# Normalizing x without the modulation, and folding scale and shift into the DFT over the hidden dimension

## The chip, the cores and the metric

The kernel runs on one core of a Trainium2 chip. Its time is the device time of the program in microseconds, the median of the runs shown. Before the change three runs gave 1993.35, 1994.33 and 1990.18 us, median 1993.35. The engines are called TensorE (PE, with its weight loads as PEld), VectorE (DVE), ScalarE (ACT), GpSimd (POOL) and SyncE (SP), as in the profile.

## What is computed

```python
# x 2048 x 1024 (S x D), w_mod 1024 x 6144, w1 1024 x 3584, w2 3584 x 1024, DFT matrices S x S and D x D
sa, ca, ga, sb, cb, gb = (silu(c) @ w_mod) in six rows of 1024
h = LN(x) * (1 + ca) + sa
x = x + ga * A(h)          # A(h) = Re(DFT over the sequence of (DFT over the hidden dimension of h))
h = LN(x) * (1 + cb) + sb
x = x + gb * (gelu(h @ w1 + b1) @ w2 + b2)
# A(h) = Wsre @ (h @ Wdre.T) - Wsim @ (h @ Wdim.T), with the four DFT matrices given as fp32 inputs
```

Everything is fp32, and the result has to be close to fp32 in accuracy.

## The kernel before, in words

**Stages.** The sequence DFT is done first (real and imaginary part of S @ h), then the DFT over d, then the two products of the MLP. TensorE works in f16: each fp32 operand is scaled by a power of two and split into a high and a low half, and each product is three passes, high by high, high by low and low by high. The high half is a cast by ACT, the low half a subtraction by DVE. Nearly all large products use a Strassen-like scheme of seven products on combined quarter blocks, so that DVE and POOL also form sums and differences of operands.

In the order of the program on TensorE:

- The start. The rows sa and ca are made by TensorE as fp32 matmuls: for each eighth k of d, four 128 x 512 products of the column silu(c), repeated 128 times, with a 1 MB piece of w_mod (`mod_pe`, L474; the last eighth in `mod_rows`, L486). Between them stand idle f16 matmuls (`idle_pe`, L480). From the rows DVE takes a maximum and a power-of-two scale (L507 to L511).
- The first stage, called plain (L1112): 16 chunks of 48 matmuls, 768 in all, the products of the first sequence-DFT quadrants with the x tiles. Chunk n = 8 ri + kp needs matrix chunk n (`c0_tasks`, split by L681 on ACT and L684 on DVE) and the halves of the x tiles.
- The second stage (L1162): 84 operands of 24 matmuls, the rest of the sequence DFT, on sums of x tiles (`s_tasks`) and sums of matrix chunks (`comb_c`, L716, split again by L681/L684).
- The third stage (L1394): the DFT over d, 1344 matmuls on the results u of the stages before and on the seven combinations of each DFT matrix over d (`d_tasks`), which go through DRAM as dc (store L828, reload `load_dp` L1359).
- The two products of the MLP (L1585, L1694), 2352 matmuls each.

**Work on x.** `x_tasks(k)` handles the tiles k and k + 8 of 128 rows: mean and variance (bn_stats on DVE for k = 0, sums on ACT for the others, L592, L601, L605), the inverse root with a Newton step on two-column tiles (L603 to L618), then for each tile (x - mean) * ca1 (L633), times r plus sa (L634), the cast (L635, ACT) and the low half (L636, DVE). Tile 0 goes through `mod_rows` by halves of 512 columns (L494, L499, L504), since it is first.

**Other rows.** `row_tasks` makes ga, sb, cb and gb on DVE in the second stage: eight loads of 512 KB, eight products with the column silu(c) accumulated in one tile (L542 for the first, L544 for the others), then an all-reduce over the partitions on POOL (L552) and a store.

**Matrices over d.** `d_tasks(n)`, n = 0 to 7, follows the rows: a 1 MB load of two row blocks (L810), split and combined in place (high half L821 on ACT with the scale SD = 16, low half L824 on DVE, differences L837, L841, L842), and stored by POOL (L828) through a ring of four staging tiles.

**What sets the order.** Each piece of such work is a Task with an engine, a modelled cost and dependencies, in one of several streams, each with a due time. While the kernel is built, `pick` and `fill_to` choose the task that can start first by modelled clocks (`clk`, `done`, `LANDS`), up to the modelled time of TensorE, whose matmuls are written out in order; `need` and `emitted` force what a matmul reads. The chip executes each engine's list in exactly that order. T0 is the modelled time at which the first stage starts. All loads are issued by SP in order, on eight completion semaphores in turn, so at most eight are outstanding; POOL issues the stores of s, u and dc.

## Time and profile before

| | |
|---|---|
| median of the runs | 1993.35 us (1990.18 to 1994.33) |
| profiled execution, its span | 1990.4 us; it lies 2.95 us under the median and inside the range of the runs |
| TensorE busy in it | 1969.1 us, 99% |
| first matmul of the first stage | 47.42 us |
| start of the second stage (L1162) | 221.68 us |
| start of the third stage (L1394) | 658.33 us |
| DVE, ACT, POOL busy | 1417.3, 851.1, 190.5 us |

A page of the profile gives in its first part the busy time of each engine, in the second the same by 40 slices of the span, in the fourth the chain of work that ended last, in the fifth the costliest groups of instructions (`line engine operation out<-in xcount | busy, mean ns of one | idle time of the engine just before them, and what ended most of it`). A row of the timeline is `start, length, engine, line, operation, count [idle before <-releaser]`. The granted clock of TensorE was 1.00 in the second stage.

### The profile page before, as it was taken

The numbers are of one execution on the slowest core, as the hardware profiler recorded it, in microseconds if no ns is written. First come the engines' busy times: TensorE is split into PE (matmuls) and PEld (weight loads), VectorE is DVE, ScalarE is ACT, GpSimd is POOL, SyncE is SP. The second block draws the span as 40 slices with busy tenths as digits, with TensorE's granted clock in tenths as the row PEclk, the third lists the DMA queues.
The fourth block names the chain that finished last, engine by engine and source line by source line (L and its number), as shares of the span: only waits on it lengthen the run. The fifth ranks groups of instructions, "written<-read, shape, count | busy, mean of one in ns | idle before, by whom it ended". The sixth has DMA issues, their size and how long they took to land. (4 is left out here: it accounts for less than half of the span.)

```text
span 1990.4 us, 23735 instructions
## 1 busy us (share of the span) xinstructions
PE 1969.1 (99%) x9082; PEld 896.5 (45%) x9082; DVE 1417.3 (71%) x1795; ACT 851.1 (43%) x1091; POOL 190.5 (10%) x282
## 2 busy tenths in 40 slices
...
DVE  2977886997984467777588999999873353553566
...
GB/s 380 53 97 281 236 264 275 246 298 329 249 256 364 271 261 256 282 244 277 276 218 190 171 199 168 145 175 146 169 231 216 117 97 83 127 101 69 111 74 85
DMA packets 139363, 402.42 MB, mean 202 GB/s; under 512 B 15536, under 2 KB 15536, under 8 KB 134640
## 3 DMA queue, kind: packets, MB, share of 16 engines
...
HBM read 262.95 MB, written 137.89 MB: 201 GB/s over the span
## 5 line engine op out<-in xcount | busy, mean ns | idle before, releaser
L1694 PE MATMUL ps<-arena 128*128 128x512 f16 x2352 | 511.1, 379 | 2.8 <-DVE arena L1740 1.5
L1585 PE MATMUL ps<-arena 128*128 128x512 f16 x2352 | 510.2, 379 | 2.2 <-ACT arena L1607 2.2
L1162 PE MATMUL ps<-arena 128*128 128x512 f16 x2016 | 435.5, 379 | 1.4 <-DMA arena<-s 1.4
L1694 PEld LDWEIGHTS <-arena 128*128 128x128 f16 x2352 | 229.9, 98 | 281.5 <-issue 3.8
L1585 PEld LDWEIGHTS <-arena 128*128 128x128 f16 x2352 | 230.1, 98 | 279.4 <-issue 2.5
L1740 DVE SCALAR_TENSOR_TENSOR arena<-ps,i4c,arena 128x1024 f32<-128x1024 f32 x179 | 229.3, 1281 | 144.4 <-PE ps L1694 143.1
L1162 PEld LDWEIGHTS <-arena 128*128 128x128 f16 x2016 | 197.1, 98 | 239.5 <-DMA arena<-s 1.9
L1394 PE MATMUL ps<-arena 128*128 128x512 f16 x1344 | 292.4, 379 | 1.9 <-DMA arena<-u 1.9
L386 ACT ACTIVATE arena<-arena,shc 128x512 f16<-128x512 f32 (+1 forms) x115 | 115.9, 1018 | 277.3 <-PE ps L1694 184.6
L1394 PEld LDWEIGHTS <-arena 128*128 128x128 f16 x1344 | 131.4, 98 | 158.0 <-DMA arena<-u 2.4
L1112 PE MATMUL ps<-arena 128*128 128x512 f16 x768 | 167.4, 379 | 7.2 <-ACT arena L635 2.0
L411 DVE TENSOR_TENSOR arena<-arena 128x512 f32<-128x512 f32 (+1 forms) x228 | 171.0, 753 | 4.1
L681 ACT ACTIVATE arena<-arena 128x1024 f16<-128x1024 f32 x100 | 104.1, 1050 | 150.8 <-PE ps L1162 111.4
L398 DVE SCALAR_TENSOR_TENSOR arena<-arena,shc 128x512 f16<-128x512 f32 (+1 forms) x115 | 128.7, 1122 | 38.4 <-ACT arena L386 38.3
L684 DVE SCALAR_TENSOR_TENSOR arena<-arena 128x1024 f16<-128x1024 f32 x100 | 128.6, 1303 | 18.5 <-ACT arena L681 18.5
L1611 DVE TENSOR_TENSOR arena<-arena,ps 128x512 f32<-128x512 f32 x84 | 57.5, 685 | 110.7 <-PE ps L1585 106.5
L1604 ACT ACTIVATE arena<-arena,b1s,i1c 128x512 f32<-128x512 f32 x84 | 68.3, 813 | 137.0 <-DVE arena L1611 137.0
L1112 PEld LDWEIGHTS <-arena 128*128 128x128 f16 x768 | 74.7, 98 | 99.9 <-ACT arena L635 4.0
L773 ACT ACTIVATE arena<-arena 128x1024 f16<-128x1024 f32 x56 | 57.7, 1047 | 60.9 <-DVE arena L1186 18.8
L776 DVE TENSOR_TENSOR arena<-arena 128x1024 f16<-128x1024 f32 x56 | 66.9, 1218 | 14.6 <-ACT arena L773 14.6
L386 ACT ACTIVATE arena<-arena,s1c 128x512 f16<-128x512 f32 (+1 forms) x70 | 60.8, 884 | 36.9 <-DVE arena L411 25.9
L398 DVE SCALAR_TENSOR_TENSOR arena<-arena,s1c 128x512 f16<-128x512 f32 (+1 forms) x70 | 66.3, 959 | 11.0 <-ACT arena L386 10.8
...
## 6 DMA issues: line engine op xcount, KB each, us to landing
...
arena<-w SPq DMA_DIRECT2D x119, 256.0 KB, 2.7
...
arena<-u SPq DMA_DIRECT2D x112, 256.0 KB, 4.0
...
```

The costliest lines, as they stand in the source:

```text
L386: act.activation(o[m][0], q(j), AF.Copy, **sc)
L398: dve.scalar_tensor_tensor(o[m][1], q(j), scale, o[m][0], op0=ALU.mult, op1=ALU.subtract)
L411: dve.tensor_tensor(q(d), q(a), q(b), op=op)
L681: h = Task("act", 1.15, lambda: act.activation(o[:, :, 0], s2, AF.Copy, scale=SC), list(deps) + free)
L684: dve.scalar_tensor_tensor(o[:, :, 1], s2, SC, o[:, :, 0], op0=ALU.mult, op1=ALU.subtract)
L1112: pe.matmul(bank_of(d_), hleft(d_, s, kp, a), cop(n)[:, s, b], start=(kp == 0 and s == 0 and a == 0 and b == 0), stop=(kp == 7 and s == 1 ...
L1162: pe.matmul(bank_of(st + ch), left, cop(n)[:, s, b], start=(start and kp == 0 and s == 0 and a == 0 and b == 0), stop=(kp == 3 and s == 1 ...
L1394: pe.matmul(bank_of(bk), up(N)[:, c_, a], dp(n)[:, c_, w], start=(start and ri == 0 and c_ == 0 and i == 0), stop=(ri == 1 and c_ == 3 and ...
L1585: pe.matmul(ps.rearrange("p (k t) -> p k t", k=4), w1c[:, m, s, a, d * P : (d + 1) * P], zc(m)[:, b, :, d, :], start=(start and d == 0 and ...
L1604: act.activation(dst, src, AF.Gelu_apprx_tanh, scale=inv, bias=b1s[:, 2 * p + j : 2 * p + j + 1])
L1694: pe.matmul(t[:, j], hidc[:, c_, m, a, k * P : (k + 1) * P], w2c[:, m, c_, w], start=(start and c_ == 0 and n == 0), stop=(c_ == 1 and n = ...
L1740: lambda: dve.scalar_tensor_tensor(dst, ps[b], inv, dst, op0=ALU.mult, op1=ALU.add), kp[b],
```

## The change

The rows sa and ca no longer scale x. LN(x) alone, times 128, is split and goes through the sequence DFT (one TENSOR_SCALAR for each tile, L624), and its column 0 is overwritten with the constant 128 (a memset of one column, L625). So column 0 of the product holds the row sums of the sequence matrices. The scale is put into the matrices over d: each row block d is multiplied by cs[d] = (1 + ca[d]) times a power of two, and from it the term of row 0 is taken off (`d0`, two scalings per matrix chunk, L817), since column 0 of LN(x) was dropped; LN(x) sums to zero over d, so that this column is minus the sum of the others. Row 0 of the matrix over d is replaced by the row A0 or A1, the product of sa with the matrix (`arow_d`, a 4 KB load into one partition).

With that go these edits:

- `mod_pe`, `mod_rows`, their eight 1 MB loads and 32 fp32 matmuls are taken out; 18 idle matmuls stay ahead of the first stage. T0, the modelled start, is 9 where it was 42. SP's first loads are those of x and of the sequence matrix.
- bn_stats on DVE are used for k = 0 and 1.
- ca, sa and ga are made by `row_tasks` (products L490, L492, all-reduce L501) during the first stage, in places of the u area; after ca and sa follow a few operations that turn each row into a column (L508, L511, L516) and make the scales (L520 to L527). `need("early")` stands ahead of the last chunk.
- In the second stage the rows are sb, A0, A1, cb, gb, five where there were four (ga, sb, cb, gb); A0 and A1 use pieces of the matrices over d and the column of sa.
- `d_tasks` takes its chunks in the order 1, 2, 3, 0; each is scaled by two SCALAR_TENSOR_TENSORs (L817) before it is split, SD is 8, the high half is a plain cast (L833), the low half a TENSOR_TENSOR (L836), and the staging ring has three tiles.

SP's list at the start of the program, before (cc is the vector c, wm is w_mod, cre the real part of the sequence matrix; `arena` is one large on-chip buffer in which all tiles lie):

```order
L1433 DMA cc_187<-in_c_dram 128x8
L1427 DMA arena_65<-in_wm_dram 128x2048 x7
L1424 DMA arena_65<-in_x_dram 128x1024 x2
L1427 DMA arena_65<-in_wm_dram 128x2048
L692 DMA arena_65<-in_cre_dram 128x2x512
L1424 DMA arena_65<-in_x_dram 128x1024 x2
L692 DMA arena_65<-in_cre_dram 128x2x512 x2
L1424 DMA arena_65<-in_x_dram 128x1024 x2
L692 DMA arena_65<-in_cre_dram 128x2x512
L1424 DMA arena_65<-in_x_dram 128x1024 x10
```

and now:

```order
L1444 DMA cc_189<-in_c_dram 128x8
L1438 DMA arena_65<-in_x_dram 128x1024 x2
L686 DMA arena_65<-in_cre_dram 128x2x512
L1438 DMA arena_65<-in_x_dram 128x1024 x2
L686 DMA arena_65<-in_cre_dram 128x2x512
L1438 DMA arena_65<-in_x_dram 128x1024 x2
L686 DMA arena_65<-in_cre_dram 128x2x512
L1438 DMA arena_65<-in_x_dram 128x1024 x2
L686 DMA arena_65<-in_cre_dram 128x2x512
L1438 DMA arena_65<-in_x_dram 128x1024 x8
L483 DMA arena_65<-in_wm_dram 128x1024 x4
```

The weights stand behind all of x and four matrix chunks, and in pieces of half the size.

DVE's list in the start before (ps is the product of the modulation rows; L684 is the low half of the first matrix chunk, L504 the low half of half a tile of x):

```order
L507 TENSOR_REDUCE mx_189<-ps 128x1 [waits PE_49] x4
L508 TENSOR_REDUCE m_5_188<-mx_189 128x1 [waits DVE_49]
L199 TENSOR_SCALAR m_5_188<-m_5_188 128x1 [waits DVE_49]
L510 RECIPROCAL m_5_188<-m_5_188 128x1 [waits DVE_49]
L511 TENSOR_SCALAR m_5_188<-m_5_188 128x1 [waits DVE_49]
L494 SCALAR_TENSOR_TENSOR arena_65<-arena_65,xmv_9_192,ps 128x512
L514 SCALAR_TENSOR_TENSOR xcl_10_193<-xcl_10_193,m_5_188 128x2 [waits DVE_49]
L499 SCALAR_TENSOR_TENSOR arena_65<-arena_65,xcl_10_193 128x512 [waits DVE_49,Activation_49]
L603 TENSOR_SCALAR xcl_12_195<-xmv_11_194 128x2
L684 SCALAR_TENSOR_TENSOR arena_65<-arena_65 128x2x512 [waits DMAHW3_49]
L504 TENSOR_TENSOR arena_65<-arena_65 128x512 [waits DMAHW5_49,Activation_49]
```

and now, from the end of the statistics of the first pair of tiles (L624 and L625 are the new normalization, L630 the low half of an x tile, L678 that of a matrix chunk, L490 the first product of the row ca):

```order
L624 TENSOR_SCALAR arena_65<-arena_65,xmv_11_196,xcl_12_197 128x1024 [waits DVE_49]
L625 MEMSET arena_65 128x1 [waits DVE_49]
L587 BN_STATS xst_10_195<-arena_65 128x6 [waits DMAHW4_49]
L490 TENSOR_SCALAR arena_65<-arena_65,scol_188 128x1024 [waits DMAHW5_49]
L630 TENSOR_TENSOR arena_65<-arena_65 128x2x512 [waits Activation_49]
L678 SCALAR_TENSOR_TENSOR arena_65<-arena_65 128x2x512 [waits DMAHW3_49]
L624 TENSOR_SCALAR arena_65<-arena_65,xmv_11_196,xcl_12_197 128x1024
L625 MEMSET arena_65 128x1 [waits DVE_49]
L598 TENSOR_SCALAR xcl_16_201<-xmv_15_200 128x2 [waits Activation_49]
L587 BN_STATS xst_10_195<-arena_65 128x6
```

The maximum over the rows and the scaling by halves are gone. The product L490, which waits for a load of SP, stands between the normalization of the first x tile and the low halves of that tile and of the first matrix chunk.

DVE's list at the first unit of the matrices over d before (L824 is the low half, L837 a difference of two quarters, L776 the split of u, L716 a sum of matrix chunks):

```order
L684 SCALAR_TENSOR_TENSOR arena_65<-arena_65 128x2x512 [waits PE_49]
L824 SCALAR_TENSOR_TENSOR arena_65<-arena_65 128x512 [waits DMAHW6_49,DMASW7_49,Activation_49]
L824 SCALAR_TENSOR_TENSOR arena_65<-arena_65 128x2x512 [waits DMASW1_49,DMASW0_49,Activation_49]
L837 TENSOR_TENSOR arena_65<-arena_65 128x512
L837 TENSOR_TENSOR arena_65<-arena_65 128x512 [waits DVE_49]
L776 TENSOR_TENSOR arena_65<-arena_65 128x4x2x128 [waits DMASW6_49]
L776 TENSOR_TENSOR arena_65<-arena_65 128x4x2x128 [waits DMASW2_49,Activation_49]
L716 TENSOR_TENSOR arena_65<-arena_65 128x1024
L684 SCALAR_TENSOR_TENSOR arena_65<-arena_65 128x2x512 [waits PE_49]
```

and now (L817 scales, L836 is the low half, L849 the difference, L678 the low half of an operand of the second stage):

```order
L678 SCALAR_TENSOR_TENSOR arena_65<-arena_65 128x2x512 [waits PE_49,Activation_49] x2
L817 SCALAR_TENSOR_TENSOR arena_65<-arena_65,cs_190 128x1024 [waits DMAHW5_49]
L817 SCALAR_TENSOR_TENSOR arena_65<-arena_65,cs_190 128x1024
L678 SCALAR_TENSOR_TENSOR arena_65<-arena_65 128x2x512 [waits PE_49,Activation_49]
L836 TENSOR_TENSOR arena_65<-arena_65 128x2x512 [waits DMASW5_49,Activation_49]
L836 TENSOR_TENSOR arena_65<-arena_65 128x512 [waits DMASW7_49,Activation_49]
L849 TENSOR_TENSOR arena_65<-arena_65 128x512
L849 TENSOR_TENSOR arena_65<-arena_65 128x512 [waits DVE_49]
```

DVE's first operation of a unit now waits for the load itself (DMAHW); before, ACT's cast did so, and DVE waited for ACT.

The diff, cut to its core:

```diff
-SD = 16.0
+ONE = 1.0
+SD = 8.0
...
-    O_ROW = (72, 76)
-    O_DS = (O_AUX + 8, O_AUX + 12, 64, 68)
+    O_ERLY, O_LATE = (184, 188, 192, 196), (O_AUX, O_AUX + 4, O_AUX + 8, O_AUX + 12)
+    O_D0 = O_AUX + 12
+    O_DS = (O_AUX + 8, 64, 68)
...
+    def row_tasks(name, places, after):
+
+        mrow = at(places[0], 1024)
+        src = {"A0": 0, "A1": 1}
         r = []
         for k in range(ND):
-            b = at(O_AUX + 4 + 4 * (k % 3), 1024)
-            l = Task(
-                "dma", 1.5, lambda k=k, b=b: sp.dma_start(b, wm[:, k, j * D : (j + 1) * D]),
-                [("row", j, k - 3) if k > 2 else ("row", j - 1, ND) if j > 2 else ("op", 15)], ("wm", j, k),
-            )
+            b = at(places[1 + k % 3], 1024)
+
+            def load(k=k, b=b):
+                if name in src:
+                    sp.dma_start(b, dri[src[name]][:, k, :])
+                else:
+                    j = ("sa", "ca", "ga", "sb", "cb", "gb").index(name)
+                    sp.dma_start(b, wm[:, k, j * D : (j + 1) * D])
+
+            l = Task("dma", 1.5, load, [("row", name, k - 3)] if k > 2 else [after] if after else [], ("wm", name, k))
+            col = csa if name in src else scol
...
+            deps = [l.key] + ([("row", "sa", "end")] if name in src else [])
...
+        def column(o):
+
+            def f():
+                dve.tensor_tensor(rows, rows, ident[:, None, :].to_broadcast([P, ND, P]), op=ALU.mult)
+
+            def g():
+                dve.tensor_reduce(o, rows, axis=AX.X, op=ALU.add)
+
+            return [("dve", 1.25, f), ("dve", 1.25, g)]
...
+            dve.tensor_scalar(cs, cs, sd, None, op0=ALU.mult)
+            dve.tensor_scalar(m1[:, 4:5], m1[:, 4:5], sd, -1.0, op0=ALU.mult, op1=ALU.mult)
+            dve.tensor_scalar(csa, csa, sd, 1.0 / ONE, op0=ALU.mult, op1=ALU.mult)
...
-        if k < 1:
+        if k < 2:
...
-            mean, op = (mv[:, n, 0:1], ALU.subtract) if k < 1 else (ss[:, n : n + 1], ALU.add)
+            mean, op = (mv[:, n, 0:1], ALU.subtract) if k < 2 else (ss[:, n : n + 1], ALU.add)
+
+            def norm(x_=x_, mean=mean, op=op, n=n):
+                dve.tensor_scalar(x_, x_, mean, r[:, n : n + 1], op0=op, op1=ALU.mult)
+                dve.memset(x_[:, 0:1], ONE * SH)
+
             u = chain(
-                ("dve", 1.3, lambda x_=x_, mean=mean, op=op: dve.scalar_tensor_tensor(x_, x_, mean, ca1s, op0=op, op1=ALU.mult)),
-                ("dve", 1.3, lambda x_=x_, n=n: dve.scalar_tensor_tensor(x_, x_, r[:, n : n + 1], sas, op0=ALU.mult, op1=ALU.add)),
+                ("dve", 0.8, norm),
...
-        ri, c_ = divmod(n, 4)
+        ri, c_ = n // 4, (1, 2, 3, 0)[n % 4]
         b = at(O_AUX, 2048).rearrange("p (h x) -> p h x", h=2)
         q = at(O_AUX, 2048).rearrange("p (q e) -> p q e", q=4)
-        l = Task("dma", 2.9, lambda: sp.dma_start(b, dri[ri][:, c_::4, :]), [("dd", n - 1)] if n else [("row", 5, ND)])
+        d0 = at(O_D0, 1024)
+        l = Task("dma", 2.9, lambda: sp.dma_start(b, dri[ri][:, c_::4, :]), [("dd", n - 1)] if n else [("row", "gb", "end")])
         LANDS[l.key] = 5.0
+        head = [l]
+        if n % 4 == 0:
+            z = Task("dma", 1.5, lambda: sp.dma_start(d0, dri[ri][0, 0].partition_broadcast(P)), l.deps)
+            w = Task("dve", 0.7, lambda: dve.tensor_scalar(d0, d0, m1[:, 4:5], None, op0=ALU.mult), [z.key], ("d0", ri))
+            head += [z, w]
+        got = []
+        for h in range(2):
+
+            def f(h=h):
+                k = c_ + 4 * h
+                dve.scalar_tensor_tensor(b[:, h], b[:, h], cs[:, k : k + 1], d0, op0=ALU.mult, op1=ALU.add)
+
+            head.append(Task("dve", 1.3, f, [l.key, ("d0", ri)]))
+            got.append(head[-1].key)
+        if c_ == 0:
+            head.append(Task("dma", 0.3, lambda: sp.dma_start(b[0:1, 0, :], arow_d[ri][:, :]), [got[0], ("row", f"A{ri}", "end")]))
+            got[0] = head[-1].key
...
-                act.activation(o[0][:, :, 0], q[:, sl], AF.Copy, scale=SD)
+                act.activation(o[0][:, :, 0], q[:, sl], AF.Copy)
 
             def lo():
-                dve.scalar_tensor_tensor(o[0][:, :, 1], q[:, sl], SD, o[0][:, :, 0], op0=ALU.mult, op1=ALU.subtract)
+                dve.tensor_tensor(o[0][:, :, 1], q[:, sl], o[0][:, :, 0], op=ALU.subtract)
...
-    T0 = 42.0
+    T0 = 9.0
...
+                if ri and kp == 7 and s == 0 and d == 0:
+                    need("early")
...
+    for k in range(8):
+        for i in (k, k + 8):
+            load_x(i).run()
+            done["x", i] = 4.0 + 1.4 * (2 * k + i // 8 + min(k, 4))
+        if k < 4:
+            c0[k][0].run()
+            done["craw", k] = 4.0 + 1.4 * (3 * k + 2)
...
+    idle_pe(18)
+    clk.update(dma=8.0, act=4.0, dve=1.5, pe=8.0)
...
-    for n, j in enumerate((2, 3, 4, 5)):
-        push("row", "row", row_tasks(j, {2: "ga", 3: "sb", 4: "cb", 5: "gb"}[j]), t_op(16) + 20.0 + 30.0 * n)
+    last = None
+    for n, name in enumerate(("ca", "sa", "ga")):
+        push("row", "early", row_tasks(name, O_ERLY, last), t_op(6) + 30.0 * n)
+        last = ("row", name, "end")
...
+    for n, name in enumerate(("sb", "A0", "A1", "cb", "gb")):
+        push("row", "row", row_tasks(name, O_LATE, last), t_op(16) + 10.0 + 24.0 * n)
+        last = ("row", name, "end")
```

178 lines of the change are left out of this document (57 added, 121 removed).

## The prediction

> **What bounds the kernel now.** I read the page from the top: its first part (busy time of each engine), DVE's row of the second (busy tenths in 40 slices), and in the fifth the group of the first DFT stage.
>
> ```profile
> PE 1969.1 (99%) x9082; PEld 896.5 (45%) x9082; DVE 1417.3 (71%) x1795; ACT 851.1 (43%) x1091; POOL 190.5 (10%) x282
> ...
> DVE  2977886997984467777588999999873353553566
> ...
> L1112 PE MATMUL ps<-arena 128*128 128x512 f16 x768 | 167.4, 379 | 7.2 <-ACT arena L635 2.0
> ```
>
> TensorE is busy for all but 21.3 us of the 1990.4 us span. Every later stage hides its preparation, so time can be gained only where TensorE is busy with something that is no product of the DFTs, and that is the start. The timeline of PE shows it, with the starts of the later stages:
>
> ```profile
> 7.13 1.96 PE L474 MATMUL ps<-arena 128*128 128x512 f32 x4 [0.17 <-DMA arena<-in_wm_dram]
> 39.91 3.60 PE L486 MATMUL ps<-arena 128*128 128x512 f32 x8
> 47.42 0.39 PE L1112 MATMUL ps<-arena 128*128 128x512 f16 x1 [0.24 <-ACT arena L517]
> 64.70 62.75 PE L1112 MATMUL ps<-arena 128*128 128x512 f16 x290 [1.07 <-DVE arena L684]
> 221.68 93.40 PE L1162 MATMUL ps<-arena 128*128 128x512 f16 x432
> 658.33 42.03 PE L1394 MATMUL ps<-arena 128*128 128x512 f16 x194
> ```
>
> From 7 to 43.5 us TensorE makes the modulation rows; the first product of the sequence DFT starts at 47.42. The 290 matmuls take 62.75 us, 0.2164 each. All 768 of that stage at this pace are 166.2 us, and it ends at 221.68: it runs as if it had started at 55.5, so 8.1 us of waits lie behind 47.42. The third stage (L1394) starts 436.65 us after the second (L1162).
>
> **The change, the start.** The 8 MB of modulation weights no longer come first, and L474, L486 and the scaling that depends on them are gone; x and the DFT matrix lead the queue. When data land, the timeline of DVE and ACT tells, by the first instructions that waited for them:
>
> ```profile
> 23.21 1.29 DVE L592 BATCH_NORM_STATS2 xst<-arena 128x6 f32<-128x512 f32 x2 [21.77 <-DMA arena<-in_x_dram]
> 28.33 1.06 ACT L681 ACTIVATE arena<-arena 128x1024 f16<-128x1024 f32 x1 [1.76 <-DMA arena<-in_cre_dram]
> 29.70 1.06 ACT L601 ACTIVATE arena<-arena 128x1024 f16<-128x1024 f32 x1 [0.31 <-DMA arena<-in_x_dram]
> ```
>
> These are the 15th, 19th and 20th half megabyte of the queue (each 1 MB load of weights counts two): 1.30 us for each, with a lead of 23.21 - 15 x 1.30 = 3.7 us. So after the change the first tile of x is there near 5, its partner near 6.3, the first chunk of the matrix near 7.6, and high halves could feed TensorE from about 12 us. That alone would start the stage some 35 us sooner.
>
> But the order of DVE's work shows one instruction in the way: the first product of the row ca (L490) stands ahead of the low half of the first x tile (L630) and of the first matrix chunk (L678), and it reads the 21st half megabyte, which lands at 29.70 + 1.30 = 31.0. DVE executes in order. Behind L490 are both low halves that the second and third pass of the first chunk need; TensorE can do a handful of high-by-high products and then waits. I therefore start DVE's ramp at 31.0, not at 12.
>
> The Trainium skill, page "DMA: Bandwidth & Descriptors", section "Where 436 GB/s comes from", says that loads from HBM are bound near 358 GB/s per core. By that, 21 x 0.524 MB would land at 3.7 + 30.8 = 34.5, and the sum below would be 3.5 us later; the rows above say 1.30 us per 0.524 MB, 403 GB/s, and I go by them.
>
> What DVE must do from there until the low half of x tile 4 is out is counted from its order and priced by the groups by form of the first 700 us:
>
> ```profile
> L542 DVE TENSOR_SCALAR arena<-arena,scol 128x1024 f32<-128x1024 f32 x4 | 3.0, 748 | 10.0 <-DMA arena<-in_wm_dram 10.0
> L544 DVE SCALAR_TENSOR_TENSOR arena<-arena,scol 128x1024 f32<-128x1024 f32 x28 | 35.8, 1280 | 19.4 <-DMA arena<-in_wm_dram 19.3
> L636 DVE TENSOR_TENSOR arena<-arena 128x1024 f16<-128x1024 f32 x15 | 18.4, 1223 | 3.5 <-ACT arena L635 3.5
> L592 DVE BATCH_NORM_STATS2 xst<-arena 128x6 f32<-128x512 f32 x4 | 2.5, 671 | 21.8 <-DMA arena<-in_x_dram 21.8
> L615 DVE TENSOR_TENSOR xcl<-xcl 128x2 f32<-128x2 f32 x8 | 1.3, 158 | 0.1
> L647 DVE TENSOR_TENSOR arena<-arena 128x512 f32<-128x512 f32 x8 | 5.5, 683 | 0.0
> L634 DVE SCALAR_TENSOR_TENSOR arena<-arena,xcl 128x1024 f32<-128x1024 f32 x15 | 19.2, 1282 | 0.3
> L635 ACT ACTIVATE arena<-arena 128x1024 f16<-128x1024 f32 x15 | 15.8, 1056 | 22.7 <-DVE arena L634 22.7
> L716 DVE TENSOR_TENSOR arena<-arena 128x1024 f32<-128x1024 f32 x48 | 62.4, 1307 | 4.4 <-DMA arena<-s 4.1
> ```
>
> Eight products for ca: 0.75 + 7 x 1.28 = 9.7. Nine low halves of x and five of the matrix at 1.22: 17.1. Nine normalizations, now one TENSOR_SCALAR each (0.75 by L542, the same form) and a one-column memset (at most a small operation, so below 0.16; I take 0.06): 7.3. Three statistics with their aggregation: 2.2. Some 37 operations on two columns at 0.16: 5.9. One subtraction at 0.69. Together 42.9 us. For comparison the removed pair L633/L634 cost 2.56 per tile, so the lighter normalization is counted in this, 1.75 saved on each tile.
>
> In that stretch lies the all-reduce of ca on POOL. What an all-reduce does to DVE, the timeline shows where one was running:
>
> ```profile
> 244.55 6.69 DVE L684 SCALAR_TENSOR_TENSOR arena<-arena 128x1024 f16<-128x1024 f32 x2
> 244.74 7.02 POOL L552 PARTITION_ALL_REDUCE arena<-arena  x1 [22.79 <-DVE arena L544]
> ...
> 342.02 7.01 POOL L552 PARTITION_ALL_REDUCE arena<-arena  x1 [34.16 <-DVE arena L544]
> 342.98 5.55 DVE L716 TENSOR_TENSOR arena<-arena 128x1024 f32<-128x1024 f32 x1
> ```
>
> An operation of 1.21 us (that is what L716 takes alone; its mean of 1.307 above includes the stretched ones) took 5.55 beside it, and two of about 1.25 took 6.69: I charge 4.35 for each all-reduce (bounds: 0, if nothing of DVE's falls beside it, to 7.0, all of it). Waits of DVE for ACT's high halves I take at 2.5 (L636 waited 3.5 in all before; 0 to 4). Ramp: 31.0 + 42.9 + 4.35 + 2.5 = 80.8. The first four chunks are 4 x 48 = 192 matmuls and two more run on the high half, so 574 x 0.2164 = 124.2 us follow: 205.0. The all-reduces of sa and ga stand in POOL's order among the stores of the sums s, whose reload the last chunks and the second stage wait for, each 7.0 us long; I add 1.5 (0 to 4). The second stage starts at 206.5 instead of 221.68: **-15.2**. Lower end of the time: no block and no waits by ACT, then the first chunk itself sets the pace, DVE delivering two low halves at 31.0 + 0.75 + 2 x 1.22 = 34.2 and the stage running as if begun at 35: 201.5, -20. Upper end: 4 for the stores and 2.5 more for the block, -10.
>
> **The change, the second stage.** Here TensorE has no gap to lose, and the question is whether DVE still keeps up:
>
> ```profile
> 380.00:440.00 60.00, 60.00 (x280) 27.20 (x279) 58.74 (x53) 30.40 (x32) 15.52 (x21) 1.00 0.66 240
> 440.00:500.00 60.00, 60.00 (x280) 27.20 (x279) 49.71 (x49) 26.71 (x28) 10.53 (x20) 1.00 0.91 340
> 500.00:560.00 60.00, 60.00 (x280) 27.20 (x279) 53.95 (x55) 32.38 (x35) 15.32 (x29) 1.00 0.67 238
> 560.00:620.00 60.00, 60.00 (x280) 27.20 (x279) 43.62 (x40) 23.90 (x25) 7.00 (x13) 1.00 0.84 302
> ```
>
> (Span, then busy time of PE, PEld, DVE, ACT, POOL.) DVE's busy time is 206.0 of 240 us; 34.0 are free. Added: 16 scalings of the matrices over d as STT, 20.5; two of the term d0, 1.5; one row more than before (five for four), 9.7, with its block 4.35. Sum 36.1, 2.1 over what is free there. It also inherits waits: the loads of these matrices were waited for by ACT, by the view of waits
>
> ```profile
> ACT arena L821 <- DMA arena<-in_dre_dram: 10.3, 3, 4.0
> ACT arena L821 <- DMA arena<-in_dim_dram: 7.4, 2, 6.9
> ```
>
> 17.7 us, and now by L817 on DVE, with low halves of the stage's own operands queued behind it (L678, for TensorE's next pieces, and u). If all of it stays bare: 2.1 + 17.7 = 19.8. If the rows spread into the free time before 380, nothing is left: 0. I take **+5**, near the low end, since in the order two low halves (2.4 us) stand between most loads' issue and L817, and before 380 there is room as well: in DVE's digits above (slices of 49.8 us), the fifth to seventh, 199 to 348, read 8, 8 and 6. The patched row (a 4 KB load) and the smaller staging ring (three buffers for four) are costed at nothing: the units are 24 us apart, and the stores they wait for land within that.
>
> The chain of rows and units must also end in time for the third stage. Before:
>
> ```profile
> 226.87 0.74 DVE L542 TENSOR_SCALAR arena<-arena,scol 128x1024 f32<-128x1024 f32 x1
> 358.80 0.75 DVE L542 TENSOR_SCALAR arena<-arena,scol 128x1024 f32<-128x1024 f32 x1 [0.46 <-DMA arena<-in_wm_dram]
> 396.14 0.56 SPq L810 DMA_DIRECT2D arena<-in_dre_dram  x1
> 565.70 0.55 SPq L810 DMA_DIRECT2D arena<-in_dim_dram  x1
> 587.33 1.22 DVE L824 SCALAR_TENSOR_TENSOR arena<-arena 128x1024 f16<-128x1024 f32 x1
> ```
>
> Rows start 44.0 apart, the last takes 37.3, units are 24.2 apart, the last ends 22.9 after its load; all done 69.8 us ahead of 658.33. After: first row 5.2 behind 206.5, then 4 x 44.0 + 37.3 + 7 x 24.2 + 22.9 gives 617; with 2.6 more per unit, 638. The third stage would start at 206.5 + 436.65 + 5 = 648. The slack shrinks from 70 to between 10 and 31 us; the reload of the products takes some of it, but I charge nothing here.
>
> **Sum.** 1990.4 - 15.2 + 5.0 = 1980.2 for a profiled execution; the median before lies 2.95 above that of its profile, so 1983.2, **1983**. Its own range: the start alone (-20 to -10) moves it to 1978 or 1988, the second stage alone (0 to 10) likewise; with part of both, 1976 to 1990.
>
> **The rivals.** One of them needs the products' way out and back, from the DMA part for the first 700 us (KB each, median us from issue to landing):
>
> ```profile
> dc<-arena POOLq DMA_DIRECT2D x56, 256.0 KB, 4.4
> arena<-dc SPq DMA_DIRECT2D x14, 1024.0 KB, 10.4
> ```
>
> A, the held product does not hold (its weights land early, or the low halves do not wait behind it). Then the stage runs as if begun near 20 (12 plus some 8 us of waits, as before): 20 + 166.2 + 1.5 = 187.7, -34, sum 1990.4 - 34 + 5 + 2.95 = 1964. Against it: DVE's order, and a queue that is in order.
> B, the block of the all-reduce and the second stage cost nothing: -20 + 0, sum 1973. For it: DVE's free time before 380, and that the block hits only an operation which happens to meet it. Against: at both all-reduces shown DVE's work was stretched by over 4 us.
> C, the second stage is DVE's: 10 to 20 us of the 19.8 come bare, sum 1988 to 1998, middle 1993, no change. For it: 58.74 busy of 60 in the first of the four windows, at the very place of the first units.
> D, slower: the third stage waits for the last products of the scaled matrices. Mechanism: each unit now waits on DVE for its load (17.7 / 8 = 2.2) and scales (2.6), 29.0 apart instead of 24.2; last unit done at 206.5 + 5.2 + 213.3 + 7 x 29.0 + 22.9 + 4.8 = 656, with 4.4 for the store and 10.4 for the reload near 671 against 643: 28 us of wait, sum 1990.4 - 15.2 + 28 + 2.95 = 2006. It decides from the point where chain and reload end more than 19 us behind 643. Against: the slack of 70 us of before, and that the planner may pack the units closer than 24.2 when they are due.
>
> **Chances.** Forecast 0.58, A 0.05, B 0.14, C 0.14, D 0.09. This kernel's measurement can tell about 0.2%, 4 us, from no change: within it is 1989.4 to 1997.3. Faster: forecast, A, B and a third of C, 0.81. Same: most of what is left of C, 0.10. Slower: D, 0.09. For the range, 1973 to 1994 holds the forecast, most of B and two thirds of C.
>
> **What would show it.** Right: DVE idle from about 11 to 31 us, released by the weights' load ahead of L490; TensorE's second burst of L1126 near 34; the first all-reduce near 70 with a DVE operation of some 5.5 us beside it; a wait of TensorE of about 4 us at chunk 4, near 80; L1176 from about 206; L1408 from 642 to 650. Wrong: no idle DVE ahead of L490 (A); L1176 after 212 (ramp underpriced); idle PE in L1176 with L678 as releaser (C); a wait at L1408 for the reload of dc, which the last unit's stores release (D).

## The result

The changed kernel takes 2010.32 us (median of four runs, 2005.9 to 2012.6) against 1992.19 us of the kernel before on the same chip: a ratio of 1.009, 95% interval 1.0073 to 1.0107. It is slower by 18 us; the prediction had it faster by 10. The profiled execution of the changed kernel has a span of 2010.8 us.

The page of the changed kernel, part 1 and the TensorE groups of part 5:

```profile
PE 1943.2 (97%) x8978; PEld 882.8 (44%) x8978; DVE 1463.0 (73%) x1854; ACT 843.6 (42%) x1078; POOL 224.2 (11%) x286
...
L1176 PE MATMUL ps<-arena 128*128 128x512 f16 x2016 | 442.1, 382 | 17.7 <-DVE arena L678 11.5
...
L1408 PE MATMUL ps<-arena 128*128 128x512 f16 x1344 | 292.9, 379 | 6.6 <-ACT arena L1424 4.1
...
L1126 PE MATMUL ps<-arena 128*128 128x512 f16 x768 | 173.8, 390 | 32.8 <-DVE arena L678 23.5
```

TensorE does 26 us less work, and waits 46 us more. 25.6 of these stand in the first stage (32.8 against 7.2), where they were forecast. The others are new: the second stage, which had waited 1.4 us, waits 17.7, most of it for low halves (L678), and the third waits 6.6 where it had waited 1.9. The timeline of PE in the changed kernel shows where (start, length, count, and in brackets the wait ahead of it with its releaser):

```profile
14.02 1.89 PE L1126 MATMUL ps<-arena 128*128 128x512 f16 x4 [6.46 <-ACT arena L629]
36.04 42.55 PE L1126 MATMUL ps<-arena 128*128 128x512 f16 x188 [20.13 <-DVE arena L678]
81.25 1.04 PE L1126 MATMUL ps<-arena 128*128 128x512 f16 x2 [2.66 <-ACT arena L629]
82.51 116.38 PE L1126 MATMUL ps<-arena 128*128 128x512 f16 x527 [0.23 <-DVE arena L630]
202.25 11.99 PE L1126 MATMUL ps<-arena 128*128 128x512 f16 x47 [3.37 <-DVE arena L678]
214.08 93.62 PE L1176 MATMUL ps<-arena 128*128 128x512 f16 x433
309.46 98.58 PE L1176 MATMUL ps<-arena 128*128 128x512 f16 x456 [1.76 <-DVE arena L678]
410.51 22.35 PE L1176 MATMUL ps<-arena 128*128 128x512 f16 x95 [2.47 <-DVE arena L678]
433.94 5.35 PE L1176 MATMUL ps<-arena 128*128 128x512 f16 x24 [1.08 <-DMA arena<-s]
441.54 12.44 PE L1176 MATMUL ps<-arena 128*128 128x512 f16 x49 [2.25 <-DMA arena<-s]
459.27 151.98 PE L1176 MATMUL ps<-arena 128*128 128x512 f16 x695 [5.30 <-DVE arena L678]
...
673.76 26.06 PE L1408 MATMUL ps<-arena 128*128 128x512 f16 x120
```

Three differences make up the 20.4 us between the two spans. The first stage ends at 214.08 instead of 221.68: -7.6. The second takes 673.76 - 214.08 = 459.7 instead of 436.65: +23.0. From the third stage's start to the end it is 2010.8 - 673.8 = 1337.0 instead of 1332.1: +5.0.

The 23.0 are more than the added waits of 16.3. Most of the difference is the pace after a wait: the 456 matmuls behind the wait of 1.76 us take 98.58 us, 0.2162 each, but the 49 behind the wait of 2.25 take 12.44, 1.85 more than 49 x 0.2162, the 95 behind 2.47 take 1.81 more, and the 695 behind 5.30 take 1.72 more. The mean granted clock was 0.987 in this run, 0.999 in the one before. The Trainium skill, page "TensorE: Matmul & The Clock Gate", section "Part 1: The HAM clock gate (the "warmup" mystery)", says that the clock falls to half after an idle window of about 3.4 us, and comes back after a busy one of that length. An estimate from that is half of 3.4 us, 1.7, for the burst behind a wait, near the 1.8 measured; but here waits from 2.25 us on paid it, and not every one did (a wait of 3.73 us in the third stage of e4, below, cost 0.13).

The start went as the prediction described it. DVE and POOL in the changed kernel:

```profile
12.82 0.06 DVE L625 MEMSET arena<- 128x1 f32 x1
32.96 0.75 DVE L490 TENSOR_SCALAR arena<-arena,scol 128x1024 f32<-128x1024 f32 x1 [19.48 <-DMA arena<-in_wm_dram]
33.63 1.22 DVE L630 TENSOR_TENSOR arena<-arena 128x1024 f16<-128x1024 f32 x1
34.76 1.22 DVE L678 SCALAR_TENSOR_TENSOR arena<-arena 128x1024 f16<-128x1024 f32 x1
...
71.20 6.99 POOL L501 PARTITION_ALL_REDUCE arena<-arena  x1 [61.69 <-DVE arena L492]
72.12 5.03 DVE L641 TENSOR_TENSOR arena<-arena 128x512 f32<-128x512 f32 x1
```

One product of the row ca holds DVE for 19.5 us, with both low halves behind it. What it waited for came at 32.96, 2 us after the 31.0 reckoned from the rows of before. The 34.5 that followed from the Trainium skill's page "DMA: Bandwidth & Descriptors" (section "Where 436 GB/s comes from") was too late by 1.5; 32.96 lies between the two. The all-reduce stretches a 0.69 us operation to 5.03.

The end of the first stage had a wait that was not forecast. POOL and DVE ahead of the last chunk:

```profile
188.77 2.21 POOL L659 DMA_DIRECT2D s<-arena  x4 [12.14 <-DVE arena L655]
191.01 6.81 POOL L501 PARTITION_ALL_REDUCE arena<-arena  x1
...
197.85 0.76 DVE L554 TENSOR_SCALAR arena<-arena,m 128x1024 f32<-128x1024 f32 x1 [6.01 <-POOL arena L501]
...
200.98 1.22 DVE L678 SCALAR_TENSOR_TENSOR arena<-arena 128x1024 f16<-128x1024 f32 x1
```

The all-reduce of ga stands in POOL's list behind four stores, so it starts at 191; DVE waits 6.0 us for it at L554, and the low half of the last matrix chunk is behind that. TensorE loses 3.4 us and then 1.8 by the clock. (What the all-reduce itself does there, without this dependency, e7 shows below.)

### The profile page after: what moved, and what is told of

Read it like the earlier page. It is cut to its first block, busy times and chain, and to the rows that moved or that the text cites. A ratio compares the mean times of both kernels' runs of the same rounds, so it can differ in the third digit from the quotient of the medians.

```text
span 2010.8 us, 23625 instructions
## 1 busy us (share of the span) xinstructions
PE 1943.2 (97%) x8978; PEld 882.8 (44%) x8978; DVE 1463.0 (73%) x1854; ACT 843.6 (42%) x1078; POOL 224.2 (11%) x286
## 5 line engine op out<-in xcount | busy, mean ns | idle before, releaser
L1176 PE MATMUL ps<-arena 128*128 128x512 f16 x2016 | 442.1, 382 | 17.7 <-DVE arena L678 11.5
L1408 PE MATMUL ps<-arena 128*128 128x512 f16 x1344 | 292.9, 379 | 6.6 <-ACT arena L1424 4.1
L1126 PE MATMUL ps<-arena 128*128 128x512 f16 x768 | 173.8, 390 | 32.8 <-DVE arena L678 23.5
L1408 PEld LDWEIGHTS <-arena 128*128 128x128 f16 x1344 | 131.3, 98 | 163.3 <-issue 4.7
L678 DVE SCALAR_TENSOR_TENSOR arena<-arena 128x1024 f16<-128x1024 f32 x100 | 128.8, 1307 | 4.0 <-ACT arena L675 4.0
L401 DVE SCALAR_TENSOR_TENSOR arena<-arena,s1c 128x512 f16<-128x512 f32 (+1 forms) x70 | 66.3, 960 | 10.5 <-ACT arena L389 10.4
```

What stands on the lines that cost most here:

```text
L401: dve.scalar_tensor_tensor(o[m][1], q(j), scale, o[m][0], op0=ALU.mult, op1=ALU.subtract)
L678: dve.scalar_tensor_tensor(o[:, :, 1], s2, SC, o[:, :, 0], op0=ALU.mult, op1=ALU.subtract)
L1126: pe.matmul(bank_of(d_), hleft(d_, s, kp, a), cop(n)[:, s, b], start=(kp == 0 and s == 0 and a == 0 and b == 0), stop=(kp == 7 and s == 1 ...
L1176: pe.matmul(bank_of(st + ch), left, cop(n)[:, s, b], start=(start and kp == 0 and s == 0 and a == 0 and b == 0), stop=(kp == 3 and s == 1 ...
L1408: pe.matmul(bank_of(bk), up(N)[:, c_, a], dp(n)[:, c_, w], start=(start and ri == 0 and c_ == 0 and i == 0), stop=(ri == 1 and c_ == 3 and ...
```

## The experiments

All numbers in one table: the median, the ratio to the kernel before on the same chip with its 95% interval, and from the profile the end of the first stage, the length of the second, and the time from the third stage's start to the end. "Units" are the eight pieces of the matrices over d, "A rows" are A0 and A1.

| kernel | median us | ratio | first ends | second | rest |
|---|---|---|---|---|---|
| before | 1992.19 | | 221.7 | 436.7 | 1332.1 |
| changed | 2010.32 | 1.0090 (1.0073 to 1.0107) | 214.1 | 459.7 | 1337.0 |
| e1 ca late | 2011.96 | 1.0104 (1.0089 to 1.0119) | 202.1 | 470.0 | 1338.6 |
| e2 scaling without wait and work | 2004.44 | 1.0061 (1.0044 to 1.0078) | 210.8 | 452.2 | 1340.6 |
| e3 scaling, work only | 2004.65 | 1.0063 (1.0047 to 1.0079) | 210.5 | 458.0 | 1336.7 |
| e4 scaling, wait only | 2007.03 | 1.0070 (1.0055 to 1.0085) | 210.0 | 457.6 | 1338.1 |
| e5 no A rows | 1989.49 | 0.9988 (0.9979 to 0.9997) | 207.4 | 443.2 | 1332.6 |
| e6 row stores on POOL | 2007.20 | 1.0078 (1.0063 to 1.0093) | 207.7 | 458.4 | 1340.1 |
| e7 ga finished by POOL | 2019.45 | 1.0139 (1.0122 to 1.0156) | 210.1 | 476.0 | 1332.1 |
| e8 = e1 + e6 + e7 | 2022.48 | 1.0156 (1.0137 to 1.0176) | 204.0 | 466.9 | 1346.2 |
| e9 no A rows, no scaling | 1982.01 | 0.9944 (0.9929 to 0.9959) | 209.3 | 436.3 | 1331.0 |
| e10 A products narrow | 2007.45 | 1.0069 (1.0053 to 1.0086) | 210.2 | 457.9 | 1340.0 |
| e11 A all-reduces out | 2002.19 | 1.0048 (1.0032 to 1.0064) | 211.3 | 452.5 | 1336.5 |
| e12 ca late, but sooner than e1 | 1993.66 | 1.0006 (0.9997 to 1.0016) | 186.6 | 466.8 | 1337.4 |
| e13 row loads overlapped | 2019.16 | 1.0146 (1.0129 to 1.0163) | 204.9 | 478.3 | 1333.5 |
| e14 = e12 + e13 | 1994.94 | 1.0015 (1.0006 to 1.0024) | 189.9 | 469.5 | 1331.6 |
| e16 A rows emptied | 2001.61 | 1.0055 (1.0039 to 1.0070) | 211.2 | 453.7 | 1338.8 |
| e17 no A rows, units late | 1992.57 | 1.0004 (0.9995 to 1.0014) | 209.1 | 448.3 | 1333.5 |
| e18 A rows inside the units, ca late | 1987.40 | 0.9978 (0.9969 to 0.9987) | 186.3 | 450.6 | 1348.8 |
| e20 = e18, units ahead of rows | 2004.51 | 1.0060 (1.0046 to 1.0074) | 184.1 | 483.2 | 1339.1 |

The profiled execution of the changed kernel ended its first stage at 214; ten other profiles whose lists are nearly the same up to there (e2 to e6, e9 to e11, e16, e17) lie between 207.4 and 211.3. So its first stage was typically some 12 us shorter than before, and a few us of the first-stage column are scatter. The stage columns are of one execution each: those of the changed kernel and of e16 lie 2.3 and 3.9 us above the median of their kernel, those of e5 and e9 4.6 and 3.6 below it. What an edit is worth in all is therefore taken from the medians; by the intervals of the ratios, a difference between two kernels of four runs each is known to some 5 us.

### The start: e1 and e12

```diff
-    last = None
+    last = ("op", 4)        # e1;  e12: ("op", 0)
     for n, name in enumerate(("ca", "sa", "ga")):
```

> Edit: the first load of the row ca waits in the plan for the low half of the fifth matrix chunk, so its products no longer stand ahead of the low halves of the first x tile. Theory (the 20.1 us wait of TensorE at 14 to 36 us is this one product, held by its load): the long burst of L1126 starts near 16 to 20 us, the second stage starts 10 to 18 us sooner than the 214 of the changed kernel, near 196 to 204, and the whole takes 1993 to 2001. Rival (DVE's work up to the end of the first stage sets its end, the hold only moved it): the early rows still need their 24 products and three all-reduces before the last chunk, the waits come back later in the stage, the second stage starts within 5 us of 214 and the whole stays above 2005.

Measured, the timeline of PE in e1:

```profile
16.33 156.53 PE L1126 MATMUL ps<-arena 128*128 128x512 f16 x717 [0.50 <-DVE arena L678]
190.37 11.94 PE L1126 MATMUL ps<-arena 128*128 128x512 f16 x47 [17.52 <-DVE arena L678]
```

The first half of the theory is shown: without that one product ahead, the long burst starts at 16.3 and 717 matmuls run in one piece. But the last chunk then waits 17.5 us for the end of the chain of the early rows. The second stage starts at 202.1, as the theory had it, yet takes 470 us and gives the gain back: 2012, as the rival had it. A stage that starts sooner gains only what the chain behind it lets through.

> Edit: the first load of the row ca waits in the plan for the low half of the first matrix chunk only, so its products follow the low halves of the first two x tiles and two matrix chunks, sooner than in the first experiment. Theory (the last chunk waits for the end of the chain of early rows, which a sooner start shortens): the wait ahead of the last chunk is between the 3.4 of the changed kernel and the 17.5 of the first experiment, the second stage starts at 195 to 203 and is as long as in the first experiment or shorter, 459 to 470; the whole 2000 to 2009. Rival: the chain ends where it did, 202, whole 2008 to 2013.

With ca a little sooner, the early rows end at 172 and the first stage at 186.6:

```profile
16.09 166.37 PE L1126 MATMUL ps<-arena 128*128 128x512 f16 x764 [0.50 <-DVE arena L678]
186.55 0.58 PE L1176 MATMUL ps<-arena 128*128 128x512 f16 x1 [4.09 <-ACT arena L1103]
194.21 96.09 PE L1176 MATMUL ps<-arena 128*128 128x512 f16 x432 [7.07 <-DVE arena L678]
```

All 764 matmuls run in one burst, and the whole is 16.7 us faster than the changed kernel, 1993.66, no different from before. This is better than either theory gave. In e12 the product stands 37 entries further back in DVE's list and waits for nothing, and 16.7 us of the 20 that it held are gained; since the lists differ later on too, not all of this need be the product's. Two waits at the second stage's start (4.1 and 7.1 us; ACT waits there 10.5 us for a store of s, with the evictions behind it) take part of the gain.

### The scaling of the matrices over d: e2, e3, e4

The 16 scalings in the changed kernel work for 1.28 us each, and the first of each unit waits for the unit's load. The lists of all engines are the same in these three as in the changed kernel.

```diff
 # e2: neither     e3: the same on whole d0 (work, no wait)     e4: b[:, h, 0:8], d0[:, 0:8] (wait, no work)
-                dve.scalar_tensor_tensor(b[:, h], b[:, h], cs[:, k : k + 1], d0, op0=ALU.mult, op1=ALU.add)
+                dve.scalar_tensor_tensor(d0[:, 0:8], d0[:, 0:8], cs[:, k : k + 1], d0[:, 0:8], op0=ALU.mult, op1=ALU.add)
```

> Edit: the 16 scalings of the matrices over d work on 8 columns of the resident tile d0, so they neither take DVE's time nor wait for the unit's load (the matrices stay unscaled; every engine's list keeps its order). Theory (both wait and work of the scaling cost): the 459.7 us from the start of the second to the start of the third stage fall by 10 to 16 us, to 444 to 450, since the waits at 309, 408 and 433 us are not of these units; whole time 1995 to 2001. Rival (the scaling is innocent, the fifth row, the all-reduces and the reloads of s cost): it stays above 455, whole time above 2006.

> Edit: the 16 scalings are done in full, 1.28 us each, but on the resident tile d0, so they do not wait for the unit's load (matrices unscaled, same order). Theory (what costs is that DVE, in order, waits for the load with low halves of the second stage behind it): close to the kernel with neither wait nor work, at most 4 us above it, 446 to 452 us between the stages. Rival (DVE's capacity: 20.5 us of work more than fits): within 4 us of the changed kernel, above 455.

> Edit: the 16 scalings touch only 8 columns of the loaded unit: DVE waits for the load as in the changed kernel, but the work is gone (matrices unscaled but for 8 columns, same order). Theory (the wait costs): within 5 us of the changed kernel, 453 to 460 us between the stages. Rival (the work costs): as the kernel with neither, 444 to 450.

Without both the second stage falls by 7.5 us, and the whole by 5.9: less than the theory's 10 to 16, and far from the 23. The 5.9 is only just clear of the noise (the ratios' intervals meet at 1.0073 to 1.0078); e9 against e5, below, gives 7.5 for the same step. With the work alone the second stage is 458.0, with the wait alone 457.6, and the medians are 2004.7 and 2007.0; the intervals of all three ratios overlap. The scaling costs some 6 to 7 us in all, and it can't be said from these runs which half of it.

### The rows A0 and A1: e5, e9, e10, e11

```diff
 # e5 (and e9, together with e2)
-    for n, name in enumerate(("sb", "A0", "A1", "cb", "gb")):
+    for n, name in enumerate(("sb", "cb", "gb")):
-        if c_ == 0:              # the copy of row 0 into the matrix
+        if c_ < 0:
 # e10: for A0 and A1 mrow[:, :8] and b[:, :8] in the products
 # e11: for A0 and A1 no partition_all_reduce
```

> Edit: the rows A0 and A1 are not made and row 0 is not patched (sa's share of the result is left out), so three rows follow in the second stage, sb, cb, gb. Theory (what is left after the scaling comes from the longer chain of rows: its products, two all-reduces, and SP and DVE waiting in order for its loads and all-reduces): the time between the starts of the second and third stage falls from 459.7 to 438 to 446, no wait of TensorE for a reload of s near 430 to 440, and the whole takes 1988 to 1997. Rival (the loss is in the units of the matrices over d, or in the late first stage): it stays above 452, the whole above 2003.

The timeline of PE in e5:

```profile
302.64 98.58 PE L1176 MATMUL ps<-arena 128*128 128x512 f16 x456 [1.00 <-DVE arena L678]
403.46 43.29 PE L1176 MATMUL ps<-arena 128*128 128x512 f16 x192 [2.25 <-DVE arena L678]
447.64 150.32 PE L1176 MATMUL ps<-arena 128*128 128x512 f16 x695 [0.89 <-DVE arena L678]
```

The waits for s near 430 and 440 and the 5.3 us ahead of 459 are gone, the third stage is back at 1332.6, and the whole is 1989.5, 20.8 us below the changed kernel. The rows are the largest part of the loss.

> Edit: neither the rows A0 and A1 (sa's share of the result is left out) nor the scaling of the matrices over d (16 scalings on 8 columns of a resident tile); what is left of the change is the new first stage and three rows in the second. Theory (these two parts carry the whole loss of the second stage): its length falls to 436.7 to 440 us from 459.7, the third stage loses nothing, the whole takes 1978 to 1985. Rival (they overlap, and either one alone takes most of the loss away): within 4 us of the kernel without A rows, 1986 to 1992.

With the scaling gone as well, the second stage is 436.3 us, as before, and its first wait of TensorE comes at 593:

```profile
209.32 383.48 PE L1176 MATMUL ps<-arena 128*128 128x512 f16 x1776
593.78 51.97 PE L1176 MATMUL ps<-arena 128*128 128x512 f16 x240 [0.98 <-DMA arena<-s]
```

So the two parts carry the whole loss of the second and third stage, and nearly add up: 20.8 + 5.9 = 26.7 of the 28.3 us between 2010.3 and 1982.0. What is left of the change, the new start with three rows in the second stage, is worth 1991.8 - 1982.0 = 9.8 us.

> Edit: the 16 products of A0 and A1 touch 8 columns each (sa's share of the result is wrong), their loads, all-reduces and stores stay, the lists of all engines keep their order. Theory (DVE's work of these products, some 19.6 us, is what the rows cost): the second stage takes 444 to 450 us, the whole 1992 to 1998. Rival (what costs is that two more rows put the units of the matrices over d 77 us later in every list, and the two all-reduces): 454 to 460, whole 2002 to 2010.

> Edit: the all-reduces of A0 and A1 are left out (row 0 of the matrices over d is wrong), all else and the order of the lists as in the changed kernel. Theory (each all-reduce holds DVE for 4.35 us): 459.7 falls by 4 to 9 us, to 451 to 456, the whole to 2000 to 2006. Rival (DVE has time for the block at those two places): at most 3 us less, 2006 to 2011.

The 16 products alone are worth 2.9 us, which is not clear of the noise, although they take DVE 19.5 (14 x 1.284 + 2 x 0.75): the theory that DVE's work is what the rows cost falls. The two all-reduces alone are worth 8.1, near twice the 4.35 that one was priced at. Together 11 of 20.8.

### What else the rows cost: e16, e17

```diff
 # e16, on top of e10 and e11 together
-                    sp.dma_start(b, dri[src[name]][:, k, :])
+                    sp.dma_start(b[:, :W], dri[src[name]][:, k, :W])        # W = 8 for A0 and A1
 # e17, on top of e5: the first unit
-        ... if n else [("row", "gb", "end")])
+        ... if n else [("row", "gb", "end"), ("op", 56)])
```

> Edit: the rows A0 and A1 stay in the lists of DVE, ACT, TensorE and SP at their places, but their products and loads cover 8 columns and their all-reduces are left out (sa's share is wrong). Theory (the place of the units, 77 us later in every list, costs what the products and all-reduces do not): the sum of the two single edits at most, 10 to 12 us below the changed kernel, whole 1997 to 2002, with the waits near 430, 450 and 605 us still there. Rival (the loads of 8 MB and the rest of the rows' traffic and work): as without the rows, 1987 to 1993.

> Edit: no rows A0 and A1 (sa's share left out), three rows, but the first unit of the matrices over d is held in the plan until the low half of operand 56, so that the units stand in DVE's list about where they stand in the changed kernel. Theory (the place of the units): 8 to 12 us slower than the kernel without A rows, 1997 to 2002. Rival (the rows themselves): within 3 us of the kernel without them, 1986 to 1993.

In e16 little of the two rows is left but their places: 16 products of 8 columns, loads of 8 columns, for which DVE still waits 6.6 us in four places, the stores and the copies of row 0, and no all-reduce. It takes 2001.6, as e11 does, and 12 us more than the kernel without the rows. Its waits stand where those of the changed kernel stand:

```profile
425.12 5.36 PE L1177 MATMUL ps<-arena 128*128 128x512 f16 x24 [1.37 <-DMA arena<-s]
431.69 5.35 PE L1177 MATMUL ps<-arena 128*128 128x512 f16 x24 [1.21 <-DMA arena<-s]
437.33 5.57 PE L1177 MATMUL ps<-arena 128*128 128x512 f16 x25 [0.28 <-DMA arena<-s]
450.48 152.60 PE L1177 MATMUL ps<-arena 128*128 128x512 f16 x695 [7.58 <-DVE arena L679]
```

So neither the work nor the 8 MB of loads nor the all-reduces of these rows make that cluster; what stays is the lists, which the planner wrote with the two rows in them. Part of it is that the units come later (first load at 427.8 in the changed kernel, at 350.8 in e5): e17 puts only the units late, at 402 (51 of the 77 us), and is 3.1 us slower than e5, with its wait at 593 us and not near 450. The rest, some 9 us, is argued and not shown: it would go with the order in which rows, units and operands stand around 400 to 460 us. In the changed kernel DVE does there, in order:

```profile
437.29 1.23 DVE L770 TENSOR_TENSOR arena<-arena 128x1024 f16<-128x1024 f32 x1 [2.96 <-ACT arena L767]
442.59 0.75 DVE L810 TENSOR_SCALAR arena<-arena,m 128x1024 f32<-128x1024 f32 x1 [4.07 <-DMA arena<-in_dre_dram]
443.38 2.48 DVE L817 SCALAR_TENSOR_TENSOR arena<-arena,cs 128x1024 f32<-128x1024 f32 x2
...
458.00 1.22 DVE L678 SCALAR_TENSOR_TENSOR arena<-arena 128x1024 f16<-128x1024 f32 x1
```

TensorE's wait of 5.3 us ends with that L678. Ahead of it stand two waits of DVE of together 7 us (the second ended with the load of row 0 for `d0`, issued at 429.07 and used 13.5 us later) and most of the first unit. Which of these would have to move was not tried by itself.

### Mends that did not work: e6, e7, e8, e13, e14

```diff
 # e6: stores of ga, sb, cb, gb, A0, A1 by gp.dma_start     e7: ga scaled and stored by POOL behind its all-reduce
 # e13: the loads of a row after the last product of the row before
-        last = ("row", name, "end")
+        last = ("row", name, ND - 1)
```

> Edit: the stores of the rows ga, sb, cb, gb, A0 and A1 are issued by POOL behind its own all-reduce, and not by SP, whose list waits 13.3 us there for the all-reduce of gb with the reloads of s and the loads of the sequence matrix behind it; the lists of TensorE, DVE and ACT are the same as in the changed kernel. Theory (SP's list held by the all-reduce makes the reloads late): the two waits for s near 430 and 440 us are gone, and part of the 5 us before 459; 459.7 falls to 450 to 455, the whole to 2001 to 2006. Rival (the reloads are late because DVE and ACT give their buffers back late, or the transfers take longer): no wait goes away, 457 to 462.

The waits for s stay (2.08 and 2.36 us, ending at 426.7 and 434.4), and 3 us in the median is within what the changed kernel's own runs scatter. SP's wait of 13.3 us for the all-reduce of gb is real in the trace and costs little.

> Edit: the row ga is multiplied with its scale and stored by POOL right behind its all-reduce, so DVE has nothing of it left to wait for ahead of the low half of the last chunk of the first stage. Theory (DVE's wait of 6.0 us for that all-reduce, with the low half queued behind it, is the wait of 3.4 us of TensorE ahead of the last chunk, and the lower clock after it the other 1.8): the second stage starts near 209 instead of 214, the whole falls by 0 to 5. Rival (the last chunk waits for other work on DVE): a wait of over 2.5 us stays there.

> Edit: the three previous mends together: the products of ca behind the fifth chunk, the row stores on POOL, and ga finished by POOL. Theory: the second stage starts near 192 to 200, its length is 452 to 465, the whole takes 1988 to 2002. Rival (the stages only trade waits, DVE's chain of rows sets the end of both): the whole stays within 5 us of the changed kernel, 2005 to 2015.

DVE no longer waits for that all-reduce, but an operation of 0.69 us beside it (L650) takes 5.17 instead, again ahead of that low half, and a wait of 2.4 us stays ahead of the last chunk. So the all-reduce holds DVE there with or without the dependency. And because the plan has other clocks from there on, the lists of DVE and ACT differ throughout the second stage: that stage gets waits of 5.8, 7.9 and 6.9 us and takes 476. The mend of a wait of 3.4 us made the kernel 9 us slower. All three together are no better.

> Edit: the loads of a row may start once the last product of the row before is done, and no longer only after its all-reduce and store (they use other buffers); nothing is left out. Theory (length of the chain of rows): the first unit's load goes out some 30 to 50 us sooner than 428, the waits near 430 and 440 us go, the third stage does not wait, the whole takes 1994 to 2002. Rival (place does not matter): 2005 to 2012.

> Edit: overlapped row loads together with the products of ca behind the low halves of the first two chunks. Theory (both gains stand): the first stage ends near 185, the second is 448 to 458 us long, the whole takes 1977 to 1988 and beats the kernel before. Rival (the second stage gives the gain of the first back, as in the first experiment): 1990 to 1996.

In e13 the chain was not shortened: the first unit's load went out at 427.05, against 427.82, though the loads were free to come sooner, and the new lists wait more (478 us). In e14, with the sooner ca, it was shortened: that load went out at 393.7, against 418.1 in e12. Yet the second stage is 2.7 us longer than in e12 and the whole no different from it (1994.9 against 1993.7), 3.5 us slower than before. Units that come 24 us sooner gained nothing there, with lists that differ in other places too. That the length of the chain is the cause is so not shown.

### A version that beats both: e18 and e20

```diff
+            def prod(h=h):                     # in the unit, ahead of the scaling
+                dve.scalar_tensor_tensor(acc_a, b[:, h], csa[:, k : k + 1], acc_a, op0=ALU.mult, op1=ALU.add)
+        if c_ == 0:                            # last unit of a matrix: all-reduce, then a copy of one row
+            head.append(Task("pool", 7.0, lambda: gp.partition_all_reduce(acc_a, acc_a, P, RED.add), [("ap1", n)], ("ar", n)))
-    O_DS = (O_AUX + 8, 64, 68)
+    O_DS = (64, 68)
```

> Edit: nothing is left out. A0 and A1 are no rows of their own: their 16 products are done inside the units, on the pieces of the matrices over d that these have loaded, into one accumulator; the all-reduce and a copy of one partition's row stand in the last unit of each matrix. The staging ring has two tiles for that, and the 8 MB of loads of the two rows are gone. The products of ca stand behind the low halves of the first two chunks. Theory (the rows' slots and their all-reduces in the middle of the stage cost, their products do not): second stage 446 to 456 us, first stage ending near 186 to 194, the whole 1975 to 1986, which beats both. Rival (the shorter ring and the all-reduce inside the unit hold the units, and DVE with 19 us more inside them): second stage above 460, the whole 1988 to 1996.

The A rows lose their places in the lists: their 16 products use the pieces that the units load anyway. With the sooner ca of e12 this takes 1987.4 us, a ratio of 0.9978 (0.9969 to 0.9987) to the kernel before, faster than both, though short of the 1975 to 1986 expected. Its timeline shows what it gained and what it lost:

```profile
193.92 230.57 PE L1192 MATMUL ps<-arena 128*128 128x512 f16 x1056 [7.07 <-DVE arena L678]
425.98 5.34 PE L1192 MATMUL ps<-arena 128*128 128x512 f16 x24 [1.49 <-DVE arena L678]
431.79 150.16 PE L1192 MATMUL ps<-arena 128*128 128x512 f16 x695 [0.46 <-DVE arena L678]
...
658.79 7.03 PE L1424 MATMUL ps<-arena 128*128 128x512 f16 x24 [3.17 <-DMA arena<-dc]
```

The cluster at 430 to 459 is gone (450.6 us for the stage). Instead the third stage waits nine times for reloads of dc, 11.8 us in all, and from its start to the end the kernel takes 16.7 us longer than before: the units, 32 to 41 us apart, with the shorter ring and the products inside them, end too late. Which of the two spreads them was not tried. That is the mechanism of the rival D, in another kernel.

> Edit: nothing is left out. As the version with A0 and A1 inside the units and the sooner ca, but the eight units stand ahead of the rows sb, cb and gb in the chain of the second stage, since those rows are read only in the third. Theory (the third stage of that version waits for dc because the units end at 618 us, behind three rows): the units end near 500, the third stage loses its 16 us of waits, the whole takes 1966 to 1978. Rival (the second stage, with the units where DVE has the sums of x and the first operands to do, loses what the third gains): 1982 to 1992.

Putting the units ahead of the rows does away with the waits for dc, as expected, but the second stage takes 483 us and the third begins with a wait of 16.9 us for u: 2004.5. The chain of rows and units has to go somewhere, and here it took the time of the sums and of u.

## Why the prediction was wrong, step by step

**The hold at the start was right.** Forecast: DVE held from about 12 to 31 us, second burst near 34, a stretched operation of 5.5 us beside the first all-reduce near 70, a wait of 4 us near 80, DVE's ramp over at 80.8. Measured: held from 13.5 to 32.96, burst at 36.04, 5.03 at 72.12, a wait of 2.66 up to 81.25, and the burst behind it at 82.51. Rival A is out by the trace, and e1 shows that the held product is the cause.

**The end of the first stage** was priced at 1.5 us for the stores of s behind the all-reduces; measured were 3.4 of wait and 1.8 of clock ahead of the last chunk, and 2.4 of clock in the burst from 82.51. The mechanism was not stores that reload late, but DVE held by the all-reduce of ga with a low half behind it: by a wait in the changed kernel, by a stretched operation in e7. So -15.2 became -7.6 in the profiled execution, and -10 to -14 in its siblings. The lower clock after waits stood in none of the terms.

**The step that failed is the +5 of the second stage**; it measured +23.0. The added work was summed rightly: DVE's busy time in that stage rose by 35.4 us, against the 36.1 of the forecast. Here are the second stage of the changed kernel and that of the kernel before (span, busy time of PE, PEld, DVE, ACT, POOL, then the granted clock, DMA's busy share and its GB/s):

```profile
214.08:673.76 459.68, 441.94 (x2017) 198.30 (x2016) 386.06 (x339) 174.83 (x180) 92.66 (x105) 0.99 0.74 264
221.68:658.33 436.65, 435.29 (x2017) 197.13 (x2016) 350.68 (x308) 172.88 (x177) 79.64 (x102) 1.00 0.76 278
```

What failed is the step from work to time: the sum was set against DVE's free time, as if that were free for anything. DVE is still idle for 73.6 us there (86.0 before), and TensorE waits all the same: the idle time was moved to other places, as waits in order, and a sum of busy times can't show that. Of the two prices, the scaling (20.5 us of work, up to 17.7 us of waits, of which "near the low end" was charged) came out near the +5 (5.9 by e2, 7.5 by e9 against e5). What was mis-sized is the fifth row, priced as 9.7 of work and 4.35 of a block, nearly all of it set off against that free time. The two rows A0 and A1 measure 20.8 in the whole kernel: 2.9 for the products, 8.1 for the all-reduces, and some 10 to 12 that neither accounts for and that stay in e16, where the rows keep their places in the lists. No run adds or removes one row alone, so the fifth row's own share is not known. (Without A0 and A1 there are three rows, one fewer than before; but the kernel before, with four, waited only 1.4 us in this stage, and e9, with three, is no shorter there.)

**"The slack shrinks, but I charge nothing"** for the third stage was also wrong by 5.0 us, though not by the reload of dc that was thought of: L1408 waits for ACT (4.1) and u (2.5, where it was 1.9 before). This loss goes with the two rows as well: from the third stage's start to the end, e5, e9 and e17, without them, take 1331.0 to 1333.5 us, as before, and e16, with the rows emptied, still takes 1338.8. The units ended at 643.7, a little past the 617 to 638 of the forecast.

**The rivals.** C (the second stage is DVE's, 10 to 20 us, 1988 to 1998) had the right stage and releaser, and was too cheap, since its 19.8 held, beside the waits of the units, only the 2.1 us by which the added work exceeded DVE's free time in 380 to 620 us. D gave 2006, near the measured 2010, for a wait for dc that does not occur in the changed kernel. That the number was close was luck; its mechanism was met in e18 and, with waits of 3 to 4 us in all, in e1 and e12. B is out by the +23.0, and e11 shows that two all-reduces alone cost 8.1.

**Open** is which rows of the lists between 400 and 460 us make the cluster of waits there; shown is that it stays when A0 and A1 are emptied in place (e16) and goes when they are taken out of the plan (e5), that later units alone bring only a small part of the loss (e17), and that it is not the rows' work.
